# Sliding-window attention and a SMELU MLP on one core: loads reordered, output quarters moved forward, masks moved to VectorE

## The chip, the cores and the metric

The kernel runs on one core of a Trainium2 chip. Its engines work through their own lists of instructions, each in order: TensorE (PE in the rows; PEld is its weight load), VectorE (DVE), ScalarE (ACT), GpSimd (POOL) and SyncE (SP). Loads from HBM are nearly all issued by GpSimd's list here, the stores of the output and the transposing copies by SyncE's. The metric is the device time of one execution in microseconds.

## The reference

Eight batches of eight heads, 576 tokens, 64 values a head. Attention sees 32 tokens to either side; its output, as 4608 rows of 512, goes through an MLP of 2048 hidden columns with a SMELU.

```python
q, k, v: (8, 8, 576, 64) float32;  w_in: (512, 2048);  w_out: (2048, 512)

scores = (q @ k.transpose(0, 1, 3, 2)) / sqrt(64)
mask   = abs(pos[:, None] - pos[None, :]) <= 32
scores = where(mask, scores, -1e9)
attn   = exp(scores - max(scores)); attn = attn / (sum(attn) + 1e-9)
x      = (attn @ v).transpose(0, 2, 1, 3).reshape(4608, 512)

h = x @ w_in
g = where(h >= 1, h, where(h <= -1, 0, (h + 1) ** 2 / 4))
out = g @ w_out                        # (4608, 512) float32
```

## The kernel before, in words

The order of all work is written out by hand. The MLP sets the beat: the 4608 tokens are 18 blocks of 256 (t), the 2048 hidden columns 8 blocks of 256 (f), and the main loop runs over slots a = 8t + f. Slot a has:

- **products** (line 433): eight matmuls give hp, 256 hidden columns for 256 tokens, from w_in and xT, the transposed attention output. hp lies in one of two PSUM buffers (ps_h); in a few early slots it borrows one of ps_o, which otherwise holds output sums.
- **SMELU** (lines 437 to 440): ScalarE writes rr = relu(0.5 h + 0.5); VectorE writes mx = max(hp, rr), then gT = min(rr, 1) * mx, bf16. So hp is free once mx is written.
- **an output quarter** (line 455): four matmuls of gT by a block of w_out, a quarter of the sum for 128 tokens. Quarter x runs in slot x + 16 (LAG): slots 0 to 15 have none, and slots 144 to 159 have nothing else. After four quarters ScalarE copies the sum out (459) and SyncE stores it (460).

The attention is done in steps put into certain slots by the tables at lines 387 to 403:

- **transposes** (tpose, 174): q and k of batches 0 to 2 are transposed on TensorE, half a batch at a time, 18 matmuls a half (9 for q's first), and copied from PSUM by ScalarE and VectorE. Later batches are transposed by SyncE's DMA.
- **scores** (212) and scores8 (239, the last 96 columns of a batch): matmuls of k by q, an exponential on ScalarE (236), then the mask of the window. The mask is a bias added by matmuls on TensorE up to slot 13 (add_mask, 205), a product on VectorE in slots 14 to 27, and from slot 28 on a product on GpSimd in four pieces of 256 columns (199 to 201).
- **sums** (266): matmuls of the exponentials by v and by ones. ScalarE takes the logarithm of the row sums (300) and the exponential of its negative (301), and VectorE multiplies this into xT (306, 309), the normalisation, which flush() puts at the head of the next slot on VectorE's list.

A batch takes five steps of scores and five of sums, spread over 18 slots. Tokens 0 to 255 of batch 0 are done before the loop; the other tokens of batch 0 come from the second half of its q and k (halves(0, 1)), loaded, transposed, scored and summed in slots 2 to 6. Slot 16 is the first that needs batch 1. The MLP's first block (slots 0 to 7) needs all of w_in, 256 columns a slot.

Before the loop GpSimd's list holds the loads in this order: k and v of batch 0's first half, w_in columns 0 to 1023, batch 0's second half mixed with w_in, then batch 1, v, w_out and batch 2 (lines 135 to 160).

Of the kernel before, what the change touches and what calls it, by code (L numbers as in the profile page):

```python
# [8 lines left out]
FP = mybir.dt.float32  # L9
# [6 lines left out]
def kernel(  # L16
# [19 lines left out]
    nc = tc.nc  # L36
# [67 lines left out]
    def load_w_in(c0, c1, h):  # L104
        nc.gpsimd.dma_start(out=w_in[64 * h:64 * h + 64, :, c0:c1],  # L105
                            in_=moe_w_in.rearrange("(h y d) f -> h d y f", h=2, d=64)[h][:, :, c0:c1])
# [25 lines left out]
    V.memset(ones, 1.0)  # L132
    for t in qTs:
        V.memset(t[:, 0:PAD], 0.0)
    for c in range(0, 1024, 256):
        for h in range(2):
            load_w_in(c, c + 256, h)

    def mix(small, large):

        for n in range(0, max(len(small), 2 * len(large)), 2):
# [3 lines left out]
    def halves(b, half):  # L145
        return [(load_long, b, half, t, y) for t in range(2) for y in range(NY)]

    mix(halves(0, 1), [(load_w_in, 1024, 1280, h) for h in range(2)] + [(load_w_in, 1280, 1536, h) for h in range(2)])
    for h in range(2):
        load_w_in(1536, 2048, h)  # L150
    mix(halves(1, 0), [(load_v, 1, 0), (load_v, 1, 1)])
    load_v(1, 2)
    load_v(1, 3)
    load_w_out(0)
    load_w_out(1)
    mix(halves(1, 1), [(load_w_out, 2)])
    load_w_out(3)
    mix(halves(2, 0), [(load_v, 2, n) for n in range(4)])
    for fn, *x in halves(2, 1):
        fn(*x)  # L160


    kT = {}
# [30 lines left out]
    pt, pt8 = {}, {}  # L194

    def mask(eng, p, m):

        if eng is P:
            for h in range(2):
                for i in range(p.shape[2]):  # L200
                    P.tensor_mul(p[:, h, i], p[:, h, i], m[:, h, i])  # L201
        elif eng is not None:
            eng.tensor_mul(p, p, m)

    def add_mask(ps, n, w):
# [162 lines left out]

    NB = NT // TB
    NF = DFF // 256
    LAG = 16
    ev, tps = {}, {}

    def at(a, *todo):
# [7 lines left out]
                yield (sums, b, y1, lo, hi), (scores, b, (y1, y1 + 1), (0, 2), (2 * k, 2 * k + 2))  # L384
        yield (sums, b, 0, MAIN, S), (scores8, b)

    at(4, (scores, 0, (0, 1), (0, 2), (2, 4)), (scores8, 0, ps_o))
    at(5, (sums, 0, 0, TB, MAIN), (scores, 0, (1, 2), (0, 2), (2, 4)))
    at(6, (sums, 0, 1, TB, MAIN, ps_s), (sums, 0, 0, MAIN, S))
    seq = [x for b in range(1, B) for x in steps(b, 224)]  # L390
    at(13, seq[0][0])
    at(14, (*seq[1][0], ps_s))
    for n, a in enumerate((21, 22, 23, 27)):
        at(a, seq[2 + n][0])
    for n, a in enumerate((12, 13, 20, 21, 22, 26, 27)):
        at(a, seq[n][1])
    sl = [30, 32, 35, 39, 42, 45, 49, 52, 56, 59, 62, 65, 69, 73, 77, 81, 84, 88, 92]
    sl += [96, 99, 103, 106, 110, 113, 116, 120, 124, 128]
    for n, a in enumerate(sl):
        at(a, seq[6 + n][0], seq[7 + n][1] if n < len(sl) - 1 else None)  # L400
    for b, half, *a in ((0, 1, 2, 3), (1, 0, 9, 11), (1, 1, 18, 19), (2, 0, 24, 25), (2, 1, 28, 29)):
        for t in range(2):
            tps[a[t]] = [(b, 2 * half + part, t) for part in range(2)]
    loads, xps = {}, {}
# [4 lines left out]
        for t in range(2):  # L409
            xps.setdefault(a + 9 + 2 * t, []).append((b, t))  # L410

    gT = {}
    for a in range(NF * NB + LAG):
        t, f = divmod(a, NF)
        eng = None if a < 14 else V if a < 28 else P
        for b, x in loads.get(a, []):
            if x < 2:
                load_nat(b, x)
# [4 lines left out]
        if t < NB:  # L423
            if f == 0:
                gT[t] = gtp.tile([128, 2 * NF, TB], BF, name="gT", tag="gT")
            r0 = TB * t % RING
            if a < LAG and a % 4 > 1 and not 3 < a < 8:
                hp = ps_o.tile([128, 2, TB], FP, name="hp", tag="op")
            else:
                hp = ps_h.tile([128, 2, TB], FP, name="hp", tag="hp")  # L430
            for j in range(2):
                for n, kk in enumerate((0, 2, 1, 3)):
                    nc.tensor.matmul(hp[:, j], w_in[:, kk, 256 * f + 128 * j:256 * f + 128 * j + 128],  # L433
                                     xT[:, kk, r0:r0 + TB], start=n == 0, stop=n == 3)

            rr = ewp.tile([128, 2, TB], FP, name="rr")
            A.activation(rr, hp, AF.Relu, scale=0.5, bias=0.5)  # L437
            mx = ewp.tile([128, 2, TB], FP, name="mx")
            V.tensor_max(mx, hp, rr)  # L439
            V.scalar_tensor_tensor(gT[t][:, 2 * f:2 * f + 2], rr, 1.0, mx, op0=ALU.min, op1=ALU.mult)  # L440
        ends = []
        for fn, *x in ev.get(a, []):
            if fn is sums:
# [3 lines left out]
                fn(*x, eng, *pool)  # L447
        for end in ends:
            end()
        if a >= LAG:  # L450
            for x in range(4 * (a - LAG), 4 * (a - LAG) + 4):
                tt, ff = divmod(x, 2 * NF)
                if ff == 0:
                    op = ps_o.tile([128, DM], FP, name="op", tag="op")
                nc.tensor.matmul(op, gT[tt // 2][:, ff, 128 * (tt % 2):128 * (tt % 2) + 128], w_out[:, ff],  # L455
                                 start=ff == 0, stop=ff == 2 * NF - 1)
                if ff == 2 * NF - 1:
                    osb = osp.tile([128, DM], FP, name="osb")
                    A.copy(osb, op)  # L459
                    nc.sync.dma_start(out=out[128 * tt:128 * tt + 128, :], in_=osb)  # L460
        if a in tps:
            copies = [tpose(b, n, t, (A.copy, V.tensor_copy)[i if a > LAG else 0], tp1((ps_s, ps_n)[i]))
                      for i, (b, n, t) in enumerate(tps[a])]
            for x in copies:
                x()
        for x in xps.get(a, []):
# [31 lines left out]
```

The softmax here doesn't subtract the row's maximum and nothing guards it: scores larger than these inputs give would overflow.

## Time and profile before

| | before |
|---|---|
| three runs, us | 335.68, 337.27, 337.89 (median 337.27) |
| profiled execution, us | 336.13 |
| span of its profile, first to last instruction, us | 334.4 |
| mean granted TensorE clock | 0.985 |
| TensorE, VectorE, ScalarE, GpSimd busy, us | 310.2, 236.2, 194.6, 160.9 |

The page gives the busy time of each engine and, in 40 slices, where it lies. Matmuls are pipelined and their recorded times overlap, so busy time of TensorE is not its work at full rate: what counts is when one group starts after the other. In a row of the timeline, the figure in brackets is the idle time of the engine ahead of the row and what ended it.

### The profile page before, as it was taken

The numbers are of one execution on the slowest core, as the hardware profiler recorded it, in microseconds if no ns is written. First come the engines' busy times: TensorE is split into PE (matmuls) and PEld (weight loads), VectorE is DVE, ScalarE is ACT, GpSimd is POOL, SyncE is SP. The second block draws the span as 40 slices with busy tenths as digits, with TensorE's granted clock in tenths as the row PEclk, the third lists the DMA queues.
The fourth block names the chain that finished last, engine by engine and source line by source line (L and its number), as shares of the span: only waits on it lengthen the run. The fifth ranks groups of instructions, "written<-read, shape, count | busy, mean of one in ns | idle before, by whom it ended". The sixth has DMA issues, their size and how long they took to land.

```text
span 334.4 us, 8639 instructions
## 1 busy us (share of the span) xinstructions
PE 310.2 (93%) x3647; PEld 203.9 (61%) x3647; DVE 236.2 (71%) x355; ACT 194.6 (58%) x320; POOL 160.9 (48%) x236
## 2 busy tenths in 40 slices
PE   8957798979999989998999999997999999999995
PEld 3535575556666656665666666664666666666642
DVE  2343888778788777886788877885788877878800
ACT  3635894766765746565656656664675666544411
POOL 8986647950155973577524953297343334000000
PEclk9976999999999999999999999999999999999999
DMA  9999999999079997699440999179941100000021
GB/s 145 133 170 151 153 159 165 162 148 79 33 163 107 87 128 157 81 89 159 104 102 33 149 129 179 61 48 166 135 105 55 44 31 34 33 31 33 31 94 63
DMA packets 122118, 34.53 MB, mean 103 GB/s; under 512 B 108768, under 2 KB 117216, under 8 KB 122080
## 3 DMA queue, kind: packets, MB, share of 16 engines
q0 software_dynamic: 93216, 18.06, 71.1%
q1 hardware_dynamic: 28864, 15.93, 18.9%
q8 instruction: 28, 0.46, 0.6%
q14 instruction: 10, 0.08, 0.1%
HBM read 36.70 MB, written 9.44 MB: 138 GB/s over the span
## 4 chain that ended last, share of the span: by engine, by line
PE 53%; POOL 23%; issue 9%; ACT 6%; DVE 4%; DMA 3%; POOLq 0%; ACTq 0%
PE op L455 24%; PE hp L433 22%; POOL pt L201 10%; POOL vn L101 5%; PE bb L294 4%; POOL kn L93 3%; POOL qn L93 2%; ACT pt L236 2%; DMA kn<-in_k_dram 2%; DMA w_in<-in_moe_w_in_dram 2%; PE tp L184 1%; PE bb L228 1%; POOL w_in L105 1%; POOL kn L85 1%; DVE mx L439 1%
## 5 line engine op out<-in xcount | busy, mean ns | idle before, releaser
L433 PE MATMUL hp<-xT,w_in 128*128 128x256 bf16 x1152 | 151.0, 275 | 3.4 <-DVE xT L306 1.9
L455 PE MATMUL op<-w_out,gT 128*128 128x512 bf16 x576 | 145.6, 380 | 0.0
L433 PEld LDWEIGHTS <-w_in 128*128 128x128 bf16 x1152 | 111.9, 98 | 45.3 <-issue 4.7
L437 ACT ACTIVATE rr<-hp 128x512 f32<-128x512 f32 x144 | 85.8, 596 | 88.6 <-PE hp L433 82.5
L439 DVE TENSOR_TENSOR mx<-hp,rr 128x512 f32<-128x512 f32 x144 | 99.2, 689 | 37.7 <-ACT rr L437 36.7
L201 POOL TENSOR_TENSOR pt<-pt,mask 128x256 bf16<-128x256 bf16 (+1 forms) x112 | 72.2, 675 | 108.0 <-ACT pt L236 85.6
L440 DVE SCALAR_TENSOR_TENSOR gT<-rr,mx 128x512 bf16<-128x512 f32 x144 | 105.4, 732 | 4.9
L455 PEld LDWEIGHTS <-gT 128*128 128x128 bf16 x576 | 53.4, 98 | 42.8
L306 DVE TENSOR_TENSOR xT<-bb,rc 128x512 bf16<-128x512 f32 (+1 forms) x32 | 21.1, 658 | 29.4 <-ACT rc L301 29.4
L236 ACT ACTIVATE pt<-bb 128x1024 bf16<-128x1024 f32 (+1 forms) x33 | 33.2, 1011 | 12.8 <-PE bb L228 11.8
L459 ACT COPY osb<-op 128x512 f32<-128x512 f32 x36 | 21.0, 583 | 17.5 <-PE op L455 17.1
L294 PE MATMUL bb<-pt,ones 64*64 64x256 bf16 (+3 forms) x352 | 21.2, 256 | 9.2 <-POOL pt L201 5.3
L101 POOL DMA_DIRECT2D vn<-in_v_dram x32 | 27.7, 890 | 0.0
L301 ACT ACTIVATE rc<-lr 128x512 f32<-128x512 f32 (+2 forms) x40 | 23.5, 589 | 1.3
L294 PEld LDWEIGHTS <-ones 64*64 64x64 bf16 x352 | 11.7, 105 | 19.0 <-issue 15.6
L300 ACT ACTIVATE lr<-bb 128x512 f32<-128x512 f32 (+2 forms) x40 | 22.0, 550 | 0.7 <-PE bb L294 0.6
L294 PE MATMUL bb<-pt,vn 64*64 64x128 bf16 (+3 forms) x712 | 19.4, 204 | 0.0
L85 POOL DMA_DIRECT2D kn<-in_k_dram x24 | 13.0, 547 | 13.0 <-DMA w_out<-in_moe_w_out_dram 6.2
L294 PEld LDWEIGHTS <-vn 64*64 64x64 bf16 x712 | 17.0, 107 | 0.0
L228 PE MATMUL bb<-qT,kT 64*64 64x128 bf16 x520 | 13.5, 217 | 0.9 <-DVE kT L187 0.8
L93 POOL DMA_DIRECT2D qn<-in_q_dram x10 | 12.4, 1250 | 0.2 <-issue 0.2
L93 POOL DMA_DIRECT2D kn<-in_k_dram x10 | 12.3, 1238 | 0.0
(45 smaller groups left out, 105.9 us busy)
## 6 DMA issues: line engine op xcount, KB each, us to landing
out_dram<-osb SPq DMA_DIRECT2D x36, 256.0 KB, 2.1
vn<-in_v_dram POOLq DMA_DIRECT2D x32, 144.0 KB, 7.8
qn<-in_q_dram POOLq DMA_DIRECT2D x10, 288.0 KB, 6.2
kn<-in_k_dram POOLq DMA_DIRECT2D x10, 288.0 KB, 8.5
w_out<-in_moe_w_out_dram POOLq DMA_DIRECT2D x4, 512.0 KB, 8.5
kn<-in_k_dram POOLq DMA_DIRECT2D x24, 72.0 KB, 4.0
w_in<-in_moe_w_in_dram POOLq DMA_DIRECT2D x12, 128.0 KB, 5.0
qn<-in_q_dram POOLq DMA_DIRECT2D x20, 72.0 KB, 6.7
```

Source lines behind the costliest of these rows:

```text
L93: nc.gpsimd.dma_start(out=x[:, :, h], in_=src[b, NY * h:NY * h + NY].rearrange("y s d -> (y s) d") .rearrange("(u p) d -> p u d", p=128))
L101: nc.gpsimd.dma_start(out=vn[b][64 * a:64 * a + 64, :, h], in_=v[b, y:y + 2].rearrange("y s d -> (y s) d") .rearrange("(c r) d -> r c d", ...
L201: P.tensor_mul(p[:, h, i], p[:, h, i], m[:, h, i])
L236: A.activation(p, ps[:, :, :128 * n].rearrange(like, y=m), AF.Exp, scale=D ** -0.5)
L294: nc.tensor.matmul(bb[HD[h], a, o + c0:o + c1], ones[HD[a]] if c is None else vn[b][HD[a], c, h], p(a, h), start=n == 0, stop=True, skip_g ...
L300: A.activation(lr[:, :, :D0], bb[:, :, D0:2 * D0], AF.Ln)
L301: A.activation(rc[:, :, :D0], lr[:, :, :D0], AF.Exp, scale=-1.0)
L433: nc.tensor.matmul(hp[:, j], w_in[:, kk, 256 * f + 128 * j:256 * f + 128 * j + 128], xT[:, kk, r0:r0 + TB], start=n == 0, stop=n == 3)
L437: A.activation(rr, hp, AF.Relu, scale=0.5, bias=0.5)
L439: V.tensor_max(mx, hp, rr)
L440: V.scalar_tensor_tensor(gT[t][:, 2 * f:2 * f + 2], rr, 1.0, mx, op0=ALU.min, op1=ALU.mult)
L455: nc.tensor.matmul(op, gT[tt // 2][:, ff, 128 * (tt % 2):128 * (tt % 2) + 128], w_out[:, ff], start=ff == 0, stop=ff == 2 * NF - 1)
```

## The change

- **Loads.** w_in's first 512 columns are followed by q of batch 0's second half, one half of the next 512 w_in columns, k of that half, and then the rest of w_in in pieces of 512 columns. w_out's first block is loaded ahead of batch 1's first half, two more right behind it, then v of batch 1, and the last block ahead of batch 1's second half.
- **Steps.** Batch 0's second half is transposed in slot 1, scored in slots 2 and 3 and summed in slots 3 to 5; the first steps of batch 1 move by one or two slots.
- **Output quarters.** A table gives the quarters of slots 11 to 15 (0 to 7; `pre` stand ahead of the slot's sums, `post` behind); from slot 16 on slot a has quarter a - 8. The loop has 152 slots in place of 160, and quarters of two output sums may be open at the same time. Only slots 6 and 7 borrow a buffer of ps_o for hp.
- **Masks.** Added on TensorE up to slot 11, multiplied by VectorE from slot 12 on; GpSimd has none.
- The words that came with the change name the SMELU's maximum in SBUF; mx is a tile in SBUF in both versions, and its lines are not in the diff.

```diff
--- before.py
+++ after.py
@@ -132,10 +132,6 @@
     V.memset(ones, 1.0)
     for t in qTs:
         V.memset(t[:, 0:PAD], 0.0)
-    for c in range(0, 1024, 256):
-        for h in range(2):
-            load_w_in(c, c + 256, h)
-
     def mix(small, large):
 
         for n in range(0, max(len(small), 2 * len(large)), 2):
@@ -145,19 +141,18 @@
     def halves(b, half):
         return [(load_long, b, half, t, y) for t in range(2) for y in range(NY)]
 
-    mix(halves(0, 1), [(load_w_in, 1024, 1280, h) for h in range(2)] + [(load_w_in, 1280, 1536, h) for h in range(2)])
-    for h in range(2):
-        load_w_in(1536, 2048, h)
-    mix(halves(1, 0), [(load_v, 1, 0), (load_v, 1, 1)])
-    load_v(1, 2)
-    load_v(1, 3)
-    load_w_out(0)
-    load_w_out(1)
-    mix(halves(1, 1), [(load_w_out, 2)])
-    load_w_out(3)
+    def put(todo):
+        for fn, *x in todo:
+            fn(*x)
+
+    w = [(load_w_in, c, c + d, h) for c, d in ((0, 256), (256, 256), (512, 512), (1024, 512), (1536, 512)) for h in range(2)]
+    x = halves(0, 1)
+    put(w[:4] + x[:4] + w[4:5] + x[4:] + w[5:])
+    mix(halves(1, 0), [(load_w_out, 0)])
+    put([(load_w_out, 1), (load_w_out, 2)] + [(load_v, 1, n) for n in range(4)])
+    mix(halves(1, 1), [(load_w_out, 3)])
     mix(halves(2, 0), [(load_v, 2, n) for n in range(4)])
-    for fn, *x in halves(2, 1):
-        fn(*x)
+    put(halves(2, 1))
 
 
     kT = {}
@@ -194,12 +189,7 @@
     pt, pt8 = {}, {}
 
     def mask(eng, p, m):
-
-        if eng is P:
-            for h in range(2):
-                for i in range(p.shape[2]):
-                    P.tensor_mul(p[:, h, i], p[:, h, i], m[:, h, i])
-        elif eng is not None:
+        if eng is not None:
             eng.tensor_mul(p, p, m)
 
     def add_mask(ps, n, w):
@@ -368,9 +358,10 @@
 
 
 
+
     NB = NT // TB
     NF = DFF // 256
-    LAG = 16
+    quarters = {11: ([], [0]), 12: ([], [1]), 13: ([], [2]), 14: ([], [4, 5]), 15: ([6], [3, 7])}
     ev, tps = {}, {}
 
     def at(a, *todo):
@@ -384,21 +375,21 @@
                 yield (sums, b, y1, lo, hi), (scores, b, (y1, y1 + 1), (0, 2), (2 * k, 2 * k + 2))
         yield (sums, b, 0, MAIN, S), (scores8, b)
 
-    at(4, (scores, 0, (0, 1), (0, 2), (2, 4)), (scores8, 0, ps_o))
-    at(5, (sums, 0, 0, TB, MAIN), (scores, 0, (1, 2), (0, 2), (2, 4)))
-    at(6, (sums, 0, 1, TB, MAIN, ps_s), (sums, 0, 0, MAIN, S))
+    at(2, (scores, 0, (0, 1), (0, 2), (2, 4)), (scores8, 0, ps_o))
+    at(3, (sums, 0, 0, TB, MAIN), (scores, 0, (1, 2), (0, 2), (2, 4)))
+    at(4, (sums, 0, 1, TB, MAIN, ps_s))
+    at(5, (sums, 0, 0, MAIN, S))
     seq = [x for b in range(1, B) for x in steps(b, 224)]
-    at(13, seq[0][0])
-    at(14, (*seq[1][0], ps_s))
-    for n, a in enumerate((21, 22, 23, 27)):
+    at(15, seq[0][0], (*seq[1][0], ps_s))
+    for n, a in enumerate((20, 22, 23, 27)):
         at(a, seq[2 + n][0])
-    for n, a in enumerate((12, 13, 20, 21, 22, 26, 27)):
+    for n, a in enumerate((11, 12, 19, 20, 22, 26, 27)):
         at(a, seq[n][1])
     sl = [30, 32, 35, 39, 42, 45, 49, 52, 56, 59, 62, 65, 69, 73, 77, 81, 84, 88, 92]
     sl += [96, 99, 103, 106, 110, 113, 116, 120, 124, 128]
     for n, a in enumerate(sl):
         at(a, seq[6 + n][0], seq[7 + n][1] if n < len(sl) - 1 else None)
-    for b, half, *a in ((0, 1, 2, 3), (1, 0, 9, 11), (1, 1, 18, 19), (2, 0, 24, 25), (2, 1, 28, 29)):
+    for b, half, *a in ((0, 1, 1, 1.5), (1, 0, 9, 10), (1, 1, 17, 18), (2, 0, 24, 25), (2, 1, 28, 29)):
         for t in range(2):
             tps[a[t]] = [(b, 2 * half + part, t) for part in range(2)]
     loads, xps = {}, {}
@@ -409,10 +400,27 @@
         for t in range(2):
             xps.setdefault(a + 9 + 2 * t, []).append((b, t))
 
-    gT = {}
-    for a in range(NF * NB + LAG):
+    gT, op = {}, {}
+
+    def quarter(x):
+
+        tt, ff = divmod(x, 4)
+        if tt not in op:
+            op[tt] = ps_o.tile([128, DM], FP, name="op", tag="op"), []
+        o, done = op[tt]
+        for j in range(4 * ff, 4 * ff + 4):
+            nc.tensor.matmul(o, gT[tt // 2][:, j, 128 * (tt % 2):128 * (tt % 2) + 128], w_out[:, j],
+                             start=not done, stop=len(done) == 2 * NF - 1, skip_group_check=True)
+            done.append(j)
+        if len(done) == 2 * NF:
+            osb = osp.tile([128, DM], FP, name="osb")
+            A.copy(osb, o)
+            nc.sync.dma_start(out=out[128 * tt:128 * tt + 128, :], in_=osb)
+
+    for a in range(NF * NB + NF):
         t, f = divmod(a, NF)
-        eng = None if a < 14 else V if a < 28 else P
+        eng = None if a < 12 else V
+        pre, post = quarters.get(a, ([], [a - NF] if a >= 2 * NF else []))
         for b, x in loads.get(a, []):
             if x < 2:
                 load_nat(b, x)
@@ -424,7 +432,7 @@
             if f == 0:
                 gT[t] = gtp.tile([128, 2 * NF, TB], BF, name="gT", tag="gT")
             r0 = TB * t % RING
-            if a < LAG and a % 4 > 1 and not 3 < a < 8:
+            if a in (6, 7):
                 hp = ps_o.tile([128, 2, TB], FP, name="hp", tag="op")
             else:
                 hp = ps_h.tile([128, 2, TB], FP, name="hp", tag="hp")
@@ -438,6 +446,8 @@
             mx = ewp.tile([128, 2, TB], FP, name="mx")
             V.tensor_max(mx, hp, rr)
             V.scalar_tensor_tensor(gT[t][:, 2 * f:2 * f + 2], rr, 1.0, mx, op0=ALU.min, op1=ALU.mult)
+        for x in pre:
+            quarter(x)
         ends = []
         for fn, *x in ev.get(a, []):
             if fn is sums:
@@ -447,20 +457,11 @@
                 fn(*x, eng, *pool)
         for end in ends:
             end()
-        if a >= LAG:
-            for x in range(4 * (a - LAG), 4 * (a - LAG) + 4):
-                tt, ff = divmod(x, 2 * NF)
-                if ff == 0:
-                    op = ps_o.tile([128, DM], FP, name="op", tag="op")
-                nc.tensor.matmul(op, gT[tt // 2][:, ff, 128 * (tt % 2):128 * (tt % 2) + 128], w_out[:, ff],
-                                 start=ff == 0, stop=ff == 2 * NF - 1)
-                if ff == 2 * NF - 1:
-                    osb = osp.tile([128, DM], FP, name="osb")
-                    A.copy(osb, op)
-                    nc.sync.dma_start(out=out[128 * tt:128 * tt + 128, :], in_=osb)
-        if a in tps:
-            copies = [tpose(b, n, t, (A.copy, V.tensor_copy)[i if a > LAG else 0], tp1((ps_s, ps_n)[i]))
-                      for i, (b, n, t) in enumerate(tps[a])]
+        for x in post:
+            quarter(x)
+        for part in (a, a + 0.5):
+            copies = [tpose(b, n, t, (A.copy, V.tensor_copy)[i if a > 15 else 0], tp1((ps_s, ps_n)[i]))
+                      for i, (b, n, t) in enumerate(tps.get(part, []))]
             for x in copies:
                 x()
         for x in xps.get(a, []):
```

The list of GpSimd, at its loads behind the first v (L105 is w_in, L85 q and k of a half batch, L101 v, L109 w_out; the last number counts equal rows). Before:

```order
L105 DMA w_in<-in_moe_w_in_dram 64x4x256 x9
L85 DMA qn<-in_q_dram 32x2x576 x2
L105 DMA w_in<-in_moe_w_in_dram 64x4x256
L85 DMA qn<-in_q_dram 32x2x576 x2
L105 DMA w_in<-in_moe_w_in_dram 64x4x256
L85 DMA kn<-in_k_dram 32x2x576 x2
L105 DMA w_in<-in_moe_w_in_dram 64x4x256
L85 DMA kn<-in_k_dram 32x2x576 x2
L105 DMA w_in<-in_moe_w_in_dram 64x4x512 x2
L101 DMA vn<-in_v_dram 64x18x64
```

And now:

```order
L105 DMA w_in<-in_moe_w_in_dram 64x4x256 x4
L85 DMA qn<-in_q_dram 32x2x576 x4
L105 DMA w_in<-in_moe_w_in_dram 64x4x512
L85 DMA kn<-in_k_dram 32x2x576 x4
L105 DMA w_in<-in_moe_w_in_dram 64x4x512 x5
L109 DMA w_out<-in_moe_w_out_dram 128x4x512
L85 DMA qn<-in_q_dram 32x2x576 x4
L85 DMA kn<-in_k_dram 32x2x576 x4
L109 DMA w_out<-in_moe_w_out_dram 128x4x512 x2
L101 DMA vn<-in_v_dram 64x18x64 x4
```

The four q loads stand behind four loads of w_in in place of nine and more, and w_out's first three blocks ahead of batch 1's v.

The list of ScalarE in the first slots, each of which has one rr (L437 before, L445 now; qT and kT are copies of transposes, pt the exponentials of scores). Before:

```order
L437 ACTIVATE rr<-hp 128x512 x3
L187 COPY qT_99<-tp 128x4x32x5
L187 COPY qT_99<-tp 128x4x32x4
L437 ACTIVATE rr<-hp 128x512
L187 COPY kT<-tp 128x4x32x5
L187 COPY kT<-tp 128x4x32x4
L437 ACTIVATE rr<-hp 128x512
L236 ACTIVATE pt<-bb 128x2x2x256
```

And now:

```order
L445 ACTIVATE rr<-hp 128x512 x2
L182 COPY qT_99<-tp 128x4x32x5
L182 COPY qT_99<-tp 128x4x32x4
L182 COPY kT<-tp 128x4x32x5
L182 COPY kT<-tp 128x4x32x4
L445 ACTIVATE rr<-hp 128x512
L226 ACTIVATE pt<-bb 128x2x2x256
```

The copies of q and k stand behind two slots' products in place of three and four, the scores' exponential behind three in place of five.

The list of VectorE in the middle of the loop, around a step with scores and sums (xT is the normalisation). Before:

```order
L439 TENSOR_TENSOR mx<-hp,rr 128x512
L440 SCALAR_TENSOR_TENSOR gT<-rr,mx 128x512
L306 TENSOR_TENSOR xT<-bb,rc 128x2x224
L439 TENSOR_TENSOR mx<-hp,rr 128x512
L440 SCALAR_TENSOR_TENSOR gT<-rr,mx 128x512
```

And now:

```order
L447 TENSOR_TENSOR mx<-hp,rr 128x512
L448 SCALAR_TENSOR_TENSOR gT<-rr,mx 128x512
L193 TENSOR_TENSOR pt<-pt,mask_94 128x2x2x256
L296 TENSOR_TENSOR xT<-bb,rc 128x2x224
L447 TENSOR_TENSOR mx<-hp,rr 128x512
```

One mask (L193) stands between a slot's gT and the normalisation ahead of the next slot.

## Rows read from the trace of the kernel before

**Rows 1.** The page: engines' busy us (share) xinstructions; granted clock in 40 slices.

```profile
PE 310.2 (93%) x3647; PEld 203.9 (61%) x3647; DVE 236.2 (71%) x355; ACT 194.6 (58%) x320; POOL 160.9 (48%) x236
...
PEclk9976999999999999999999999999999999999999
```

**Rows 2.** Stretches, us: busy us (xinstructions) by engine, clock, DMA share, GB/s.

```profile
core 0: us, PE busy (x) PEld busy (x) DVE busy (x) ACT busy (x) POOL busy (x), PEclk, DMA share, GB/s
14.86:30.06 15.20, 9.01 (x78) 6.16 (x76) 5.92 (x9) 5.11 (x8) 12.03 (x22) 0.68 1.26 159
30.06:38.46 8.40, 6.08 (x161) 4.67 (x161) 5.83 (x10) 7.59 (x14) 7.48 (x12) 0.97 1.40 148
90.00:315.00 225.00, 219.73 (x2480) 147.40 (x2479) 175.96 (x254) 135.66 (x226) 105.11 (x144) 1.00 0.80 92
```

**Rows 3.** Timeline of TensorE: start us, us, instruction [idle before, releaser].

```profile
17.61 1.03 PE L433 MATMUL hp<-xT,w_in 128*128 128x256 bf16 x8 [0.44 <-DMA w_in<-in_moe_w_in_dram]
...
21.81 1.17 PE L184 MATMUL tp<-ident,qn 128*64 128x128 bf16 x18 [3.17 <-DMA qn<-in_q_dram]
...
27.14 1.17 PE L184 MATMUL tp<-ident,kn 128*64 128x128 bf16 x18 [2.34 <-DMA kn<-in_k_dram]
...
28.24 1.89 PE L433 MATMUL hp<-xT,w_in 128*128 128x256 bf16 x8
...
30.06 0.63 PE L208 MATMUL bb<-bias,ident 64*64 64x512 bf16 x4
...
40.30 0.69 PE L184 MATMUL tp<-ident,qn 128*64 128x128 bf16 x18
...
40.92 1.92 PE L433 MATMUL hp<-xT,w_in 128*128 128x256 bf16 x16
...
52.09 0.82 PE L433 MATMUL hp<-xT,w_in 128*128 128x256 bf16 x6 [1.48 <-DVE xT L306]
```

**Rows 4.** Loads of w_in, then one of k: ns min/median/max, first and last start.

```profile
L105 POOL DMA_DIRECT2D w_in<-in_moe_w_in_dram x4: 620/637/659, 9.0 to 10.8; - x4
...
DMA to landing us min/median/max: 4.6/4.8/5.0
...
L85 POOL DMA_DIRECT2D kn<-in_k_dram x1: 535/535/535, 19.8 to 19.8; - x1
...
DMA to landing us min/median/max: 3.3/3.3/3.3
```

**Rows 5.** Waits of TensorE, 90:331 us, then 52.5:90: us, times, longest.

```profile
PE bb L294 <- POOL pt L201: 5.3, 7, 1.3
...
PE bb L294 <- DVE xT L306: 1.8, 2, 1.2
```

**Rows 6.** Groups: xcount | busy us, mean ns | idle; L440 last at 108:124.

```profile
L439 DVE TENSOR_TENSOR mx<-hp,rr 128x512 f32<-128x512 f32 x144 | 99.2, 689 | 37.7 <-ACT rr L437 36.7
...
L437 ACT ACTIVATE rr<-hp 128x512 f32<-128x512 f32 x144 | 85.8, 596 | 88.6 <-PE hp L433 82.5 <-DVE pt L203 1.7 <-DVE gT L440 1.5
...
L201 POOL TENSOR_TENSOR pt<-pt,mask 128x256 bf16<-128x256 bf16 x88 | 61.5, 729 | 85.6 <-ACT pt L236 85.6
...
L203 DVE TENSOR_TENSOR pt<-pt,mask 128x1024 bf16<-128x1024 bf16 x4 | 2.7, 686 | 0.0
...
L203 DVE TENSOR_TENSOR pt<-pt,mask 128x384 bf16<-128x384 bf16 x1 | 0.4, 359 | 0.0
...
L440 DVE SCALAR_TENSOR_TENSOR gT<-rr,mx x144: 691/692/1148, 17.7 to 317.1; 128x512 bf16<-128x512 f32 x144
...
L440 DVE SCALAR_TENSOR_TENSOR gT<-rr,mx 128x512 bf16<-128x512 f32 x7 | 5.8, 834 | 0.2
```

**Rows 7.** Timeline around a step with scores and sums: ScalarE, then VectorE.

```profile
195.14 1.02 ACT L236 ACTIVATE pt<-bb 128x1024 bf16<-128x1024 f32 x1 [0.87 <-PE bb L228]
...
197.24 0.62 DVE L306 TENSOR_TENSOR xT<-bb,rc 128x448 bf16<-128x448 f32 x1 [1.52 <-ACT rc L301]
```

**Rows 8.** The chain of waits, its last long piece: start us, us, what.

```profile
315.69 14.69 PE op L455 x68
```

## Prediction

> **What bounds the kernel now.** I read the busy shares first, then stretches, then the waits inside them. TensorE is busy in 310.2 of 334.4 us, VectorE in 236.2, and the granted clock is below full in the third and fourth of the 40 slices only [rows 1]. So the time is TensorE's list of work plus the places where it stands or runs slowly. The stretches [rows 2] show where these are. Between 14.86 us (first MLP product) and 30.06 TensorE is busy in 9.01 of 15.20 us at a mean clock of 0.68; up to 38.46 in 6.08 of 8.40; between 90 and 315 in 219.73 of 225. The reader should see two different losses: a large one in 24 us at the start, and a thin one, 5 us, over the long middle.
>
> The start is resolved in the rows of TensorE [rows 3]. The third product (slot 2) is over at 18.6; the transposes of q's second half of batch 0 begin at 21.81, after 3.17 us of waiting for its load; those of k at 27.14, after 2.34 us more. Both sets take 1.17 us where the same 18 take 0.69 at 40.30, and eight products take 1.89 us where they take 1.03 at 17.61: they run at 1.2 GHz. Only then, at 30.06, come the scores of batch 0's second half, on which all else of batch 0 hangs. In the middle, TensorE waits 5.3 us in 7 places for a mask on GpSimd, and between 52.5 and 90 us 1.8 us for a normalised xT (the buffer of the sums is free only then) [rows 5].
>
> **The change, part by part.**
>
> *Loads of batch 0's second half.* GpSimd's queue serves its loads one after the other. The fourth w_in load is issued at 10.8 and lands 5.0 us later, at 15.8; the sixth of the eight q and k loads is issued at 19.8 and lands 3.3 us later, at 23.1 [rows 4]. Between these landings lie seven w_in loads of 128 KB and six of 72 KB, 1328 KB in 7.3 us: 182 KB a us. In the new queue four q loads (288 KB) stand right behind the fourth w_in load: the last lands at 15.8 + 1.6 = 17.4. A 256 KB w_in load and four k loads follow: 20.4. The other half of the w_in columns of slots 2 and 3: 21.8. The rest of w_in, 1 MB: 27.4.
>
> *Slots 0 to 2.* The products of slots 0 and 1 end at 17.2 as now. q's transposes run from 17.4, k's from 20.4, slot 2's products from 21.8 to 22.7 at full clock (0.87, see slots 11 to 15). The scores follow, some 7.3 us before their 30.06, but the products of slots 3 and 4, done by then today, are still to come.
>
> *Slots 3 to 10.* Here VectorE sets the pace: a slot costs it 0.69 (mx) + 0.69 (gT) = 1.38 us [rows 6], and products go at most two slots ahead, as hp has two buffers. Slot 2's maximum starts at 22.7 + 0.60 (rr) + 0.7 for the pipeline and the hand-overs = 24.0; slot 8's six slots later, with three normalisations of 0.6 us in between, at 24.0 + 8.3 + 1.8 = 34.1. Slot 10's products start when it ends, at 34.8, against 40.92 now [rows 3]: 6.1 us sooner with the same work done. w_in lands in time for this (slot 6 runs at about 28).
>
> *Slots 11 to 15, with eight quarters.* Four matmuls of a quarter cost 4 x 0.216 (68 take 14.69 us at the end [rows 8]) = 0.86 us, eight 6.9 us; they leave the end, where only such matmuls run. From slot 10's start to slot 16's TensorE has six slots of products at 8 x 0.108 = 0.87 (half the columns of an output matmul), the eight quarters, 18 transposes at 0.69, two steps of scores and two of sums, together some 15 us, and I find two waits of about 1 us (scores for k's copies; slot 16 for both normalisations, 1.48 us now [rows 3]): slot 16 starts at 34.8 + 17.0 = 51.8. Now it starts in full at 52.09 with two of its eight products done before, 51.9. So slot 16 starts where it did, with 6.9 us of work behind it that now stands at the end. That takes w_out's blocks in time: by the rate above (512 KB, 2.8 us) and the new order they land at about 32, 38, 41 and 48, the second batch's v at 45; they are wanted at 39, 41, 43 and 49, v at 48. The margin is 0.5 to 3 us, and TensorE takes its list in order, so a late block is paid in full.
>
> *The clock at the start.* The rows show it halved after a wait of 3.2 us behind one of 0.4; the new kernel still waits 2.3 us between q's and k's transposes. The cost of half a clock on the work behind it is bounded by 0 (no fall) and by what [rows 3] show at half: 0.5 for a set of transposes, 0.86 for each of some three slots, 3.1 us. I take one set and one slot, 1.4, being nearer to the row of today's shorter waits. The Trainium skill ("TensorE: Matmul & The Clock Gate", What's actually happening) says that the throttled state is the default and activity lifts it, and that the place of the change shifts from run to run; by it the 2.3 us of waiting would cost something in one run and nothing in the next, so the sum would be anything between both ends. The trace agrees in that the clock fell after the waits. **Start: 6.9 - 1.4 = 5.5 us gained** (bounds 2 and 8).
>
> *Masks on VectorE.* 88 masks of 256 columns at 729 ns (and 24 short ones) leave GpSimd, four of them being one of 1024 columns at 686 ns on VectorE: 22 x 0.69 + 6 x 0.36 = 17.3 us more for an engine busy in 176 of the 225 us [rows 2, 6]. A mask is ready after 0.69 us in place of 2.9, and no load stands in front of it, so TensorE's 5.3 us of waiting for it should go; I keep 0.3 for the hand-over: **5.0 us gained** (bounds 3 and 6). What covers the 17.3 us is seen in a step with scores and sums [rows 7]: VectorE stands 1.52 us before the normalisation, waiting for ScalarE's logarithm and exponential, while the scores' exponential is done at 196.16; a mask of 0.69 fits into that idle time. If that cover is gone, each mask delays the next maximum by its length; see the rivals. There is relief too: with masks on GpSimd the gT operation takes 834 ns on average, at least 692 without [rows 6]; this is off the path and counts for nothing. GpSimd's loads lose masks in front of them; they land well before use, nothing either.
>
> *Shifted steps.* The second batch's sums move from slots 21 and 22 to 20 and 22, so that the first normalisation is over before the buffer is wanted: **1.2 us** of the 1.8. One step of scores (slot 12 in place of 13) no longer gets its mask by matmuls on TensorE, 0.63 us at half clock [rows 3]: **0.3 us**. The maximum is written to an SBUF tile in both versions; that part changes nothing.
>
> **Sum:** 5.5 + 5.0 + 1.2 + 0.3 = 12.0 us. The profiled execution took 336.13 us, 1.1 below the median of the runs shown; 336.1 - 12.0 = 324.1 us.
>
> **The rivals.**
>
> *Late loads or a slow clock at the start.* If w_out or v land 2 to 3 us later than by the rate, or the clock stays down for three slots, the start brings 1 to 2 us in place of 5.5: about 328. For it: margins of 0.5 to 3 us, and landings in [rows 4] whose time from issue varies from 3.3 to 5.0 us. Against: the bytes in front of each of these loads are nearly the same as now.
>
> *Masks eat their own gain.* TensorE's waits for masks turn into equal waits for VectorE, which then carries 193 us in some 219 (88%) and takes its list in order: only the start's gain is left, and a little of that is lost as hp buffers come free later: 330 to 335, taken as 333.
>
> *Slower.* The mask stands in VectorE's queue behind gT and ahead of the next maximum. If the idle time of [rows 7] doesn't cover it, all 17.3 us arrive on TensorE through the two hp buffers: 324.1 + 17.3 = 341. It decides from where the idle time in a slot with scores falls under 0.69 us; the row has 1.52, but steps with scores and no sums have no logarithm to wait for.
>
> *The quarters don't fit.* If slots 11 to 15 stay bound by copies and maxima, the quarters there only replace idle time (as forecast); if not, they push slot 16 back by what doesn't fit, and nothing is lost against now, as they are gone from the end. So this has no slower side.
>
> **How the numbers follow.** Forecast 324.1 with 0.66; loads or clock late, 328, 0.16; masks eat their gain, 333, 0.11; slower, 341, 0.07. The forecast's own range is 320 (start 8, masks 6, the rest as above) to 327. The range given, 319 to 331, takes in the first rival and about a third of the second, and leaves out under 2 in 10. A measurement of this kernel can tell about 1% from no change, 334 to 340.6. Faster: the forecast, the first rival and nearly half of the second, 0.86; same: the other part and a little of the third, 0.08; slower 0.06.
>
> **What would show it.** q's transposes at about 17.5 and k's at 20.5, the clock below full for less than the present 10 us; the first output quarter before 40 and eight before slot 16's products at about 52; a pure run of output matmuls at the end of 7 us; no wait of TensorE for a mask above 0.3 us; VectorE's idle time before its normalisations smaller by a mask each. Wrong would be: TensorE waiting for w_out or v between 38 and 50, waits of ScalarE or TensorE for gT or mx in the middle, or a stretch from 90 us on that is busy less than 97%.

## The result, and the profile after

The changed kernel takes 324.79 us (median of four runs, 324.12 to 325.42) against 337.39 (four runs): 0.964 of the time, 95% interval 0.961 to 0.967. The forecast was 324.1, in a range of 319 to 331. The profiled execution took 325.0 us (its span is 323.2), 11.1 less than the profiled one before; the medians lie 12.6 apart.

The page of the changed kernel (busy time of each engine, the granted clock in 40 slices, then gT and the normalisation on VectorE) and the same three kinds of stretch as in [rows 2], columns as there:

```profile
PE 307.1 (95%) x3643; PEld 202.6 (63%) x3643; DVE 246.7 (76%) x384; ACT 194.4 (60%) x320; POOL 86.2 (27%) x120
...
PEclk9987999999999999999999999999999999999999
...
L448 DVE SCALAR_TENSOR_TENSOR gT<-rr,mx 128x512 bf16<-128x512 f32 x144 | 99.6, 692 | 4.9
...
L296 DVE TENSOR_TENSOR xT<-bb,rc 128x512 bf16<-128x512 f32 (+1 forms) x32 | 21.1, 658 | 11.9 <-ACT rc L291 11.4
```

```profile
14.86:30.06 15.20, 10.70 (x157) 7.44 (x155) 5.99 (x9) 7.22 (x12) 8.99 (x16) 0.78 1.17 175
30.06:38.46 8.40, 6.61 (x116) 5.41 (x115) 6.93 (x12) 6.47 (x14) 6.76 (x10) 1.00 1.03 148
90.00:303.00 213.00, 211.99 (x2473) 143.04 (x2471) 181.34 (x275) 133.03 (x223) 24.77 (x24) 1.00 0.78 90
```

TensorE's list is the same but for one step's added mask; it is busy for 211.99 of 213 us of the long middle, against 219.73 of 225. VectorE has 10.5 us more, not 17.3. Most of the difference is gT: it takes 692 ns on average with no masks on GpSimd beside it, where [rows 6] show 834 in a stretch with them. And VectorE's idle time ahead of its normalisations is 11.9 us; the page of before has:

```profile
L306 DVE TENSOR_TENSOR xT<-bb,rc 128x512 bf16<-128x512 f32 (+1 forms) x32 | 21.1, 658 | 29.4 <-ACT rc L301 29.4
```

17.5 us of idle time, nearly all of it waiting for ScalarE's reciprocals, are gone, and 17.3 of masks came: by these sums they went into that idle time, as the step of [rows 7] let expect. The starts of the slots' products bear it out. Compared slot by slot with the kernel before, from slot 23 on only slot 74 loses time, and that to a copy of k (below), not to a mask.

The start, from TensorE's timeline (start us, us, instruction, idle ahead and its releaser):

```profile
17.08 0.69 PE L179 MATMUL tp<-ident,qn 128*64 128x128 bf16 x18
...
21.09 0.69 PE L179 MATMUL tp<-ident,kn 128*64 128x128 bf16 x18 [3.32 <-DMA kn<-in_k_dram]
...
22.74 1.87 PE L441 MATMUL hp<-xT,w_in 128*128 128x256 bf16 x8 [0.96 <-DMA w_in<-in_moe_w_in_dram]
...
24.54 0.64 PE L198 MATMUL bb<-bias,ident 64*64 64x512 bf16 x4
...
38.98 1.03 PE L441 MATMUL hp<-xT,w_in 128*128 128x256 bf16 x8 [0.72 <-DVE mx L447]
...
42.36 1.04 PE L412 MATMUL op<-w_out,gT 128*128 128x512 bf16 x4
...
52.44 1.90 PE L412 MATMUL op<-w_out,gT 128*128 128x512 bf16 x8
...
55.24 0.81 PE L441 MATMUL hp<-xT,w_in 128*128 128x256 bf16 x6 [0.69 <-DVE xT L296]
...
56.76 1.04 PE L441 MATMUL hp<-xT,w_in 128*128 128x256 bf16 x8
```

q's transposes run at 17.08, k's at 21.09, slot 2's products at 22.74 and the scores at 24.54, against 21.81, 27.14, 17.61 and 30.06 [rows 3]. Slot 10's products start at 38.98 against 40.92, the first output quarter runs at 42.36, the last two of the eight from 52.44, none of them behind a wait for w_out, and slot 16's products go on at 55.24 (before: 52.09). With 6.9 us of work moved ahead of it, the start brought 6.9 - 3.15 = 3.7 us in these two executions.

The last long piece of the chain of waits is now half as long ([rows 8]: 14.69):

```profile
311.51 7.79 PE op L412 x36
```

For the rest I take slot 17's products, since none of the slots before is a clean mark, to the end of the last output matmul. In the kernel before slot 17 starts here (timeline of TensorE):

```profile
53.60 1.04 PE L433 MATMUL hp<-xT,w_in 128*128 128x256 bf16 x8
```

From 53.60 to 315.69 + 14.69 = 330.38 are 276.8 us. After, from 56.76 to 311.51 + 7.79 = 319.30, are 262.5; with the 6.9 us that no longer stand there 269.4, so **7.4 us** were gained behind slot 17. Slot by slot these are 1.2 us up to slot 23 (the shifted sums), then 1.8, 1.8, 0.8 and 2.5 in front of slots 46, 63, 82 and 100, where TensorE had waited for masks, less 0.8 in front of slot 74.

The 3.7 us of the start are less well known, as they rest on one pair of executions. In the three traces with the old start (before, and the two runs below with masks alone moved) slot 17 starts at 53.60, 51.30 and 55.96 us; in the four with the new start (changed kernel twice, masks back on GpSimd, copy of k earlier) at 56.76, 55.82, 55.05 and 55.99. By the medians the start brought more: 12.6 less the 7.4 behind slot 17, some 5.2 us.

### The profile page after: what moved, and what is told of

The parts are those of the page before. It is cut to its first block, busy times and chain, and to the rows that moved or that the text cites. A ratio compares the mean times of both kernels' runs of the same rounds, so it can differ in the third digit from the quotient of the medians.

```text
span 323.2 us, 8537 instructions
## 1 busy us (share of the span) xinstructions
PE 307.1 (95%) x3643; PEld 202.6 (63%) x3643; DVE 246.7 (76%) x384; ACT 194.4 (60%) x320; POOL 86.2 (27%) x120
## 4 chain that ended last, share of the span: by engine, by line
PE 80%; DMA 6%; DVE 5%; ACT 3%; POOL 3%; issue 1%; POOLq 0%; ACTq 0%
PE op L412 36%; PE hp L441 35%; PE bb L284 5%; DMA w_in<-in_moe_w_in_dram 3%; DMA kT<-kn 3%; PE bb L218 2%; DVE mx L447 2%; DVE gT L448 1%; PE tp L179 1%; POOL vn L101 1%; POOL kn L85 1%; DVE xT L296 1%; ACT lr L290 1%; ACT rc L291 1%; ACT pt L226 1%
## 5 line engine op out<-in xcount | busy, mean ns | idle before, releaser
L445 ACT ACTIVATE rr<-hp 128x512 f32<-128x512 f32 x144 | 85.5, 595 | 92.3 <-PE hp L441 88.3
L448 DVE SCALAR_TENSOR_TENSOR gT<-rr,mx 128x512 bf16<-128x512 f32 x144 | 99.6, 692 | 4.9
L296 DVE TENSOR_TENSOR xT<-bb,rc 128x512 bf16<-128x512 f32 (+1 forms) x32 | 21.1, 658 | 11.9 <-ACT rc L291 11.4
L101 POOL DMA_DIRECT2D vn<-in_v_dram x32 | 27.5, 881 | 6.7 <-PE bb L218 5.9
L193 DVE TENSOR_TENSOR pt<-pt,mask 128x1024 bf16<-128x1024 bf16 (+1 forms) x34 | 21.0, 616 | 0.6 <-ACT pt L226 0.6
L284 PE MATMUL bb<-pt,ones 64*64 64x256 bf16 (+3 forms) x352 | 19.8, 258 | 1.5 <-DVE xT L296 0.6
L284 PE MATMUL bb<-pt,vn 64*64 64x128 bf16 (+3 forms) x712 | 18.5, 206 | 0.0
L284 PEld LDWEIGHTS <-ones 64*64 64x64 bf16 x352 | 10.5, 106 | 10.6 <-issue 9.6
L85 POOL DMA_DIRECT2D kn<-in_k_dram x24 | 13.1, 559 | 11.7 <-DMA w_in<-in_moe_w_in_dram 4.1
L93 POOL DMA_DIRECT2D kn<-in_k_dram x10 | 12.1, 1225 | 13.2 <-DMA kT<-kn 11.1
```

The source lines that it names most:

```text
L93: nc.gpsimd.dma_start(out=x[:, :, h], in_=src[b, NY * h:NY * h + NY].rearrange("y s d -> (y s) d") .rearrange("(u p) d -> p u d", p=128))
L101: nc.gpsimd.dma_start(out=vn[b][64 * a:64 * a + 64, :, h], in_=v[b, y:y + 2].rearrange("y s d -> (y s) d") .rearrange("(c r) d -> r c d", ...
L284: nc.tensor.matmul(bb[HD[h], a, o + c0:o + c1], ones[HD[a]] if c is None else vn[b][HD[a], c, h], p(a, h), start=n == 0, stop=True, skip_g ...
L296: muls.append(lambda: V.tensor_mul(o, bb[:, :, :D0], rc[:, :, :D0]))
```

## The experiments

**Masks back on GpSimd.**

```diff
-eng = None if a < 12 else V
+eng = None if a < 12 else V if a < 28 else P      # P: four pieces of 256 columns
```

> The changed kernel with the masks from slot 28 on GpSimd in four pieces, as before; all else as changed. If TensorE's waits for masks (5.3 us before) are what the move to VectorE took away, they come back: 330 to 332 us, with waits of TensorE for GpSimd's pt between 90 and 300 us of 4 to 7 us in sum. If the gain in the middle has another source (order of steps, output quarters with a lag of 8), the time stays at 324.5 to 326.

330.91 us (0.981 of before, 0.976 to 0.987), 6.1 more than the changed kernel. TensorE's waits between 90 and 325 us (sum, times, longest) are those of [rows 5] to the tenth:

```profile
PE bb L288 <- POOL pt L195: 5.3, 7, 1.3
```

So the masks' place is worth some 6 us, and nothing else in the change removes these waits. In this execution the clock also fell behind the last two of them (granted 0.92 and 0.91 in 225 to 235 and 235 to 245 us); in the kernel before, behind the same two waits, it stayed at 1.00.

**The masks alone**, in the kernel before.

```diff
-eng = None if a < 14 else V if a < 28 else P
+eng = None if a < 14 else V
```

> The kernel before with one edit: masks on VectorE from slot 14 to the end, none on GpSimd. If the masks are worth what was forecast, 330 to 332 us (5 to 6.5 off the time before), and VectorE's idle time takes them in. If VectorE pays for them on the path, 335 or more. If part of the middle's gain needs the earlier output quarters too, 333 to 335.

328.80 us (0.975, 0.968 to 0.982), better than expected (the kernel before, run beside it: 337.17). Slot 17 and the last piece of the chain:

```profile
51.30 1.04 PE L433 MATMUL hp<-xT,w_in 128*128 128x256 bf16 x8
...
306.44 14.69 PE op L455 x68
```

51.30 to 321.13 are 269.8 us, 7.0 less than before, though the waits that went sum to 5.3 in [rows 5]. Slot by slot the gain lies in four places, 1.8 us in front of slot 46, 1.8 of 63, 0.8 of 82 and 2.5 of 100, just where the seven waits are, recorded as 1.3, 1.3, 0.5 and 2.1: each wait cost 0.2 to 0.3 us more than its record. My reading of this is that a row's idle time counts from the recorded end of the matmul ahead, which comes later than the moment from which the next could have started (slot 17's eight products, begun at 53.60 in the kernel before, are recorded as 1.04 us, and the next group starts at 54.47, 0.87 later). The start of this kernel is the old one; that it is 1.4 us further below before than its middle explains is within the spread of the start.

**Eight steps' masks alone**, those right behind loads in GpSimd's list, in the kernel before.

```diff
+eng = ... V if a < 28 or a in (39, 42, 56, 59, 77, 81, 96, 99) else P
```

> The kernel before with the masks of slots 39, 42, 56, 59, 77, 81, 96 and 99 alone on VectorE, the steps right behind the loads of batches 4 to 7 on GpSimd's list; the others stay on GpSimd. If TensorE's waits come from masks that stand behind loads in GpSimd's list (3.4 us for v, 2.4 for q or k), nearly the whole gain of all masks on VectorE is there: 328.5 to 331 us. If it is the length of a mask on GpSimd itself (2.9 us against 0.69), or the slower gT beside it, only a third: 333 to 335.5.

329.36 us (0.978, 0.974 to 0.983), the whole gain with eight of the steps from slot 28 on. In the kernel before the chain of waits runs through such a place (start us, us, what), and through three more like it:

```profile
111.92 2.43 POOL kn L93 x2
114.35 3.41 POOL vn L101 x4
117.76 3.48 POOL pt L201 x4
```

Slot 17 and the last piece of the chain with the eight masks moved:

```profile
55.96 1.04 PE L433 MATMUL hp<-xT,w_in 128*128 128x256 bf16 x8
...
311.10 14.69 PE op L455 x68
```

55.96 to 325.79 are 269.8 us, as with all masks moved. Slot by slot the gain lies in the same four places, and TensorE waits for no mask any more. So what it had waited for was not the 2.9 us of a mask on GpSimd alone but a mask that stood behind loads in GpSimd's list; the other steps' masks were ready in time where they were. Nor was it the slower gT, which still takes 716 ns on average here.

**No early quarters.**

```diff
-pre, post = quarters.get(a, ([], [a - NF] if a >= 2 * NF else []))
+pre, post = [], [a - 16] if a >= 16 else []       # loop of 160 slots
```

> The changed kernel with the old lag of 16: no output quarter before slot 16, sixteen slots of nothing else at the end; loads, steps and masks as changed. If TensorE had idle time for only a part of the eight quarters in slots 11 to 15 (slots bound by VectorE at 1.4 us against 1.73 with a quarter), slot 16 starts 4 to 5 us sooner and the end is 6.9 us longer: 326.5 to 328.5. If all eight lay in idle time, 331 to 332. If they are worth nothing, 324.5 to 325.5.

329.02 us (0.976, 0.970 to 0.983): 4.2 us more, a little above the first range. TensorE in front of slot 16 and at slot 17:

```profile
50.53 0.38 PE L441 MATMUL hp<-xT,w_in 128*128 128x256 bf16 x2 [2.04 <-DVE xT L296]
...
51.26 1.44 PE L441 MATMUL hp<-xT,w_in 128*128 128x256 bf16 x6 [0.36 <-DVE xT L296]
...
54.20 1.06 PE L441 MATMUL hp<-xT,w_in 128*128 128x256 bf16 x8
```

Slot 17 starts 2.6 us sooner than in the changed kernel, and 6.9 us come back at the end. So about 4.3 of the 6.9 us of quarters lay in time that TensorE loses without them: here it waits 2.04 us in one piece, and six products take 1.44 us in place of 0.81 behind it, as the clock falls once more (granted 0.50 from 52 to 54 us). The other 2.6 us push slot 16 back, where the expectation had 4 to 5.

**Batch 0's second half as before.**

```diff
-put(w[:4] + x[:4] + w[4:5] + x[4:] + w[5:])       # transposes in slot 1, scores 2 and 3, sums 3 to 5
+put(w[:8]); mix(halves(0, 1), w[8:]); ...         # transposes 2 and 3, scores 4 and 5, sums 5 and 6
-if a in (6, 7):                                   # hp borrows a buffer of ps_o
+if a in (2, 3):
```

> The changed kernel with batch 0's second half as before: loaded behind half of w_in and mixed with the rest, transposed in slots 2 and 3, scored in 4 and 5, summed in 5 and 6; w_out's loads, quarters and masks as changed. If the earlier second half is worth the two waits of 3.2 and 2.3 us at the start, 327 to 329 us. If the quarters in slots 11 to 15 take up the later start (they run when w_out is there in any case), 325 to 326.5.

327.07 us (0.971, 0.968 to 0.974): the earlier second half is worth 2.3 us. The waits for q and k are back, and slots 8 and 10 start where they did before:

```profile
22.22 0.69 PE L180 MATMUL tp<-ident,qn 128*64 128x128 bf16 x18 [3.16 <-DMA qn<-in_q_dram]
...
27.13 1.08 PE L180 MATMUL tp<-ident,kn 128*64 128x128 bf16 x18 [3.23 <-DMA kn<-in_k_dram]
...
38.46 1.91 PE L441 MATMUL hp<-xT,w_in 128*128 128x256 bf16 x16 [1.07 <-DVE xT L300]
...
40.92 1.05 PE L441 MATMUL hp<-xT,w_in 128*128 128x256 bf16 x8
```

**k ahead of w_in.**

```diff
-((0, 256), (256, 256), (512, 512), (1024, 512), (1536, 512)) ... put(w[:4] + x[:4] + w[4:5] + x[4:] + w[5:])
+((0, 256), (256, 256), (512, 256), (768, 256), (1024, 512), (1536, 512)) ... put(w[:4] + x + w[4:])
```

> The changed kernel with k of batch 0's second half loaded right behind q, ahead of the w_in columns of slots 2 and 3, and these in pieces of 256 columns again. Theory: the start is set by the loads (TensorE waits 3.3 us for k, then 1.0 us for w_in, and the clock halves for 6.8 us); k lands at about 18.4, slot 2's columns at 20, the waits shrink to 1 to 2 us and the clock stays up or is halved for a shorter time: 321 to 323 us. Rival: from slot 3 on ScalarE and VectorE set the pace by themselves, and what the loads win is lost in front of slot 8: 324 to 325.5.

323.11 us (0.959, 0.954 to 0.965), 1.7 below the changed kernel's median; the intervals overlap. The timeline of TensorE shows why it is not more:

```profile
19.57 0.69 PE L179 MATMUL tp<-ident,kn 128*64 128x128 bf16 x18 [1.73 <-DMA kn<-in_k_dram]
...
26.92 1.03 PE L441 MATMUL hp<-xT,w_in 128*128 128x256 bf16 x8 [1.92 <-DMA w_in<-in_moe_w_in_dram]
...
35.67 1.03 PE L441 MATMUL hp<-xT,w_in 128*128 128x256 bf16 x8 [0.68 <-DVE mx L447]
...
44.84 0.38 PE L412 MATMUL op<-w_out,gT 128*128 128x512 bf16 x1 [1.70 <-DMA w_out<-in_moe_w_out_dram]
```

k's transposes come at 19.57, slot 10 at 35.67, 3.3 us sooner. But the waits move on along the loads: 1.92 us for w_in in front of slot 4, 1.70 for w_out in slot 12. The clock stayed up in this execution (granted 1.00 from 22 to 28.8 us).

**The same with the quarters one slot later** (0 in slot 12, 1 in 13, 2 and 4 in 14, the others in 15):

> k of batch 0's second half ahead of w_in's columns 512 and on (323.1 us so far, with a wait of 1.9 us for w_out in slot 12), and the early quarters one slot later: 0 in slot 12, 1 in 13, 2 and 4 in 14, 5, 6, 3 and 7 in 15. If w_out's landing is what holds the quarters there, that wait goes and the time is 321 to 322.5. If slot 15, with four quarters, pushes slot 16 back by as much, 322.8 to 324.

323.40 us (0.961, 0.958 to 0.965), inside the second range, but its trace shows another reason. Slots 4, 10 and 17:

```profile
28.41 1.03 PE L441 MATMUL hp<-xT,w_in 128*128 128x256 bf16 x8 [1.69 <-DMA w_in<-in_moe_w_in_dram]
...
37.16 1.03 PE L441 MATMUL hp<-xT,w_in 128*128 128x256 bf16 x8 [0.72 <-DVE mx L447]
...
55.16 1.04 PE L441 MATMUL hp<-xT,w_in 128*128 128x256 bf16 x8
```

The wait for w_out is gone, and slot 15 with four quarters does not take it back: from slot 10 to slot 17 are 18.0 us, against 19.6 in the run above (35.67 to 55.31). The time was lost earlier. Slot 4 had to wait for w_in until 28.41, 1.5 us later than in the run above, and slot 10 starts 1.5 us later. As the loads landed differently in the two executions, what the later quarters are worth by themselves stays open.

**Matmuls on zeros in the wait for k.**

```diff
+if part == 1.5:
+    keep_warm(12, ps_h, "hp")                     # between the transposes of q and of k
```

> The changed kernel with 12 matmuls on zeros (2.6 us) between the transposes of q and of k in slot 1, where TensorE waits 3.3 us for k; they delay nothing. If half a clock behind that wait costs what the trace shows (6.8 us at 1.2 GHz, 2 to 3 us of delay at slot 10), the granted clock stays at 2.4 GHz, slot 10's products start 1.5 to 3 us sooner and the time is 322 to 323.5 us. If slots 3 to 10 are paced by ScalarE and VectorE whatever the clock, 324.3 to 325.3.

323.97 us (0.963, 0.960 to 0.966), 0.8 below the changed kernel, intervals overlapping. Stretch 22 to 28.8 us in the changed kernel, then in this one, with slot 10's start (columns as in [rows 2]; the clock is the third figure from the right):

```profile
22.00:28.80 6.80, 6.06 (x80) 3.97 (x84) 1.72 (x3) 3.61 (x7) 2.96 (x6) 0.50 1.22 194
```

```profile
22.00:28.80 6.80, 5.35 (x127) 3.93 (x121) 2.89 (x5) 6.08 (x11) 3.36 (x7) 1.00 1.24 205
...
36.26 1.03 PE L441 MATMUL hp<-xT,w_in 128*128 128x256 bf16 x8 [0.72 <-DVE mx L447]
```

The clock stayed at 2.4 GHz and slot 10 starts at 36.26, 2.7 us sooner. Of six executions four had a mean clock of 0.998 or more (322.9 to 324.2 us), two of 0.992 and 0.993 (325.2, 324.9). The clock's price is there, but matmuls on zeros in that one wait do not always save it.

**SyncE's copy of k one slot earlier.** The next three ran with the changed kernel on the same chip.

```diff
-xps.setdefault(a + 9 + 2 * t, []).append((b, t))
+xps.setdefault(a + 9 + t, []).append((b, t))
```

> The changed kernel itself, unedited, on the same chip as the next three, for direct comparison: 324 to 325.5 us.

324.61 us (0.965, 0.962 to 0.968). The copy earlier, alone:

> The changed kernel with SyncE's transposing copy of k (batches 3 to 7) one slot earlier, in front of the output store that it stands behind on SyncE's list. In the changed kernel TensorE waits 0.8 us for it once, near 177 us (up to 1.7 in other versions), where GpSimd's loads now run beside it. If the copy's late issue is the cause, the wait goes and the time falls by 0.5 to 1.2 us against the changed kernel; if it is the collision with the loads alone, no change.

323.22 us (0.961, 0.958 to 0.964): 1.4 less, intervals overlapping. In the changed kernel a wait is left between 90 and 325 us that the kernel before did not have, for a transposing copy. Here it is in the first profiled execution and in that of the unedited run just above, then SyncE's list, GpSimd's load beside it, and the copy's time from issue to landing, all from the first:

```profile
PE bb L218 <- DMA kT<-kn: 0.6, 1, 0.6
```

```profile
PE bb L218 <- DMA kT<-kn: 1.2, 1, 1.2
```

```profile
159.44 2.81 SPq L186 DMA_TRANSPOSE qT<-qn  x1
...
166.78 0.33 SPq L418 DMA_DIRECT2D out_dram<-osb  x1
...
167.28 4.62 SPq L186 DMA_TRANSPOSE kT<-kn  x1
```

```profile
166.46 2.45 POOL L93 DMA_DIRECT2D qn<-in_q_dram  x2 [19.29 <-DMA qT<-qn]
```

```profile
DMA to landing us min/median/max: 10.2/10.2/10.2
```

The copy of k stands behind an output store that waits for its sum, and once it is issued it lands 10.2 us later, beside q loads that GpSimd issues as soon as q's own copy has freed their buffer (at 166.46 us; in the kernel before, behind masks, at 182.62). One slot earlier it goes ahead of the store:

```profile
158.67 2.79 SPq L186 DMA_TRANSPOSE qT<-qn  x1
...
161.63 3.47 SPq L186 DMA_TRANSPOSE kT<-kn  x1
...
166.01 0.33 SPq L418 DMA_DIRECT2D out_dram<-osb  x1
```

```profile
DMA to landing us min/median/max: 5.4/5.4/5.4
```

It lands in 5.4 us, and TensorE's wait is gone. Against the unedited run above, this kernel gains 1.3 us behind slot 17, all of it in front of slot 74, where the wait was: the 1.4 us are this one wait. Both causes named in the expectation go with the same edit, so it does not tell them apart.

**Both edits**, k first and the copy earlier, and **the same with seven matmuls on zeros**:

> k of batch 0's second half ahead of w_in's columns 512 and on (in pieces of 256 columns for slots 2 and 3), and SyncE's copy of k one slot earlier. If the two gains add, 321.5 to 322.8 us; if only the loads' order is worth something, 323 to 323.5.

> The same with 7 matmuls on zeros (1.5 us) between the transposes of q and of k, where TensorE waits for k. If the clock still falls there in a part of the executions, their times come together at the fast ones: 321 to 322.5 us with a narrower spread; if k's earlier load already keeps it up, the same as without them.

321.88 us (0.958, 0.955 to 0.961), 2.7 below the changed kernel on the same chip, and its interval lies clear of the changed kernel's: this version beats the changed kernel and the one before. With the matmuls on zeros 322.30 (0.959, 0.956 to 0.962), the same; the spread was not narrower (321.4 to 324.2).

## Why the prediction held, and where its terms were off

- **Loads, slots 0 to 2.** Order and places as forecast, a little late: k's transposes 21.1 (20.4), slot 2's products 22.7 (21.8), scores 24.5 (22.7). The rate of 182 KB a us was too high for the first 256 KB load of w_in: issued at 13.4 us, it landed 6.0 later, at 19.4, where the rate gives 18.8. w_out's blocks landed at about 31, 38, 41 and 48 us and v at 45, as forecast; but the rate alone gives 30, 36, 39, 45 and 42, so the forecast's figures do not follow from its own working.
- **Slots 3 to 10, the step whose size failed.** The forecast let VectorE run from slot 2's maximum to slot 8's in 10.1 us, paced by its own 1.38 us a slot. It took 13.0 (VectorE's timeline, slots 2 and 3, the first normalisation, slot 8):

```profile
25.27 0.69 DVE L447 TENSOR_TENSOR mx<-hp,rr 128x512 f32<-128x512 f32 x1 [5.58 <-ACT rr L445]
...
28.46 0.69 DVE L447 TENSOR_TENSOR mx<-hp,rr 128x512 f32<-128x512 f32 x1 [1.77 <-ACT rr L445]
...
31.40 0.62 DVE L296 TENSOR_TENSOR xT<-bb,rc 128x448 bf16<-128x448 f32 x1 [1.52 <-ACT rc L291]
...
38.24 0.68 DVE L447 TENSOR_TENSOR mx<-hp,rr 128x512 f32<-128x512 f32 x1
```

  VectorE stood 1.77 us for slot 3's rr and 1.52 for a reciprocal: ScalarE has the scores' exponentials in front of both, and TensorE was at half clock. With the clock up (the matmuls on zeros) the same stretch is 11.1 us, 1.0 over the forecast, as VectorE still waits there for an rr and a reciprocal. So the clock cost some 2 to 2.7 us here, not the 1.4 taken, and inside the bounds of 0 to 3.1; and ScalarE's part in the pace, put at nothing, cost about 1. Slot 10's products start at 38.98, not at 34.8 + 1.4 = 36.2.
- **Slots 11 to 15.** From slot 10's products to slot 16's in full 16.3 us (17.0 forecast), no wait for w_out or v. The first output quarter came at 42.36, not before 40 as the forecast's sign had it. Early quarters are worth 4.2 us by leaving them out, the loads' order 2.3 by undoing it.
- **Start in sum:** 5.5 forecast, bounds 2 and 8, and 0.3 for the added mask of slot 12, which also lies here and which no run measures alone. 3.7 us between the two profiled executions, some 5.2 by the medians: how far the sum was off is not settled. Of the rival with late loads and a slow clock, the clock came and the late loads of w_out and v did not.
- **Masks:** 5.0 forecast; measured 6.9 slot by slot behind slot 17, in the changed kernel and alone, and 6.1 by the medians when put back. The term was read from a row of waits that counts too little. The forecast named both the mask's 2.9 us and the loads in front of it; the run with eight steps shows that the loads decided.
- **Cover on VectorE:** held. The rivals in which masks eat their gain, or slow the kernel, did not happen: TensorE waits for no mask behind 90 us.
- **Shifted sums:** 1.2 forecast, 1.2 gained up to slot 23; the wait of 1.2 us for the first normalisation is gone. The maximum in SBUF changed nothing, as forecast.
- **"GpSimd's loads lose masks in front of them ... nothing either" was wrong:** a load that runs sooner lies beside a transposing copy, and a wait of 0.6 to 1.2 us came of it, 0.8 to 1.3 counted from slot to slot.

That the total came out so near is in part luck. In the profiled executions (325.0 against 324.1) a shortfall of 2.1 us up to slot 17 (3.7 against 5.5 + 0.3) and a surplus of 1.2 behind it (7.4 against 5.0 + 1.2) partly cancel; and the surplus is itself 1.9 too little for the masks less the 0.8 for the copy of k that was put at nothing.

## What to carry to other kernels

Work that must be ready soon should not share an in-order list with loads that take a microsecond each to issue; moving just the pieces that stand behind loads can be enough. Idle time ahead of a row understated here what TensorE lost (5.3 us recorded, 6.9 gained), so price a wait from one start to the next. And when an engine loses work, look at what its remaining transfers will then run beside.

## What the runs showed of the hardware that was not expected

- Executions of one kernel differ along with the mean granted clock, which in the profile of the kernel before is below full only at the start: it took 337.3 to 338.2 us at 0.979, and 335.6 to 336.7 at 0.988 or 0.989, on one chip. Loads land at different times too (slot 4's w_in 1.5 us apart in two executions with the same loads). A single profile is one such draw.
- A transposing copy of k took 10.2 us to land when issued 0.8 us behind two loads of q, 5.4 when issued 4 us ahead of them. With masks alone moved it is up to 9.3 us, in the unedited second run 10.7; in the kernel before, where those loads come later, no such copy takes more than 6.4.
